# First batch of a frequency-domain mixer: the layout of the buffer between the two short sums, turned from channels-inside to columns-inside

## The chip, the cores and the metric

The kernel runs on one core of one Trainium2 chip. The metric is the device time of one execution in microseconds (us). Timings of the kernel before come from three runs; one further execution was taken with the hardware profiler, and every duration below is from that one.

## The reference, cut to what matters

Two blocks run one after the other on `x` of shape (8, 3008, 256), that is batch, sequence, channels, all in float32:

```python
# block 1: a filter along the sequence, in the frequency domain
X = np.fft.rfft(x, axis=1)
Y = X * (filt_r + 1j * filt_i)[None]
y = np.fft.irfft(Y, n=x.shape[1], axis=1)
# block 2: token mixing, then channel mixing
h = np.maximum(y.transpose(0, 2, 1) @ w_tok1, 0.0) @ w_tok2
u = y + h.transpose(0, 2, 1)
out = u + np.maximum(u @ w_ch1, 0.0) @ w_ch2
```

The sequence length 3008 is 47 x 64, and the kernel computes the Fourier transform in two short sums: one of length 64 and one of length 47, each as matrix products with tables of cosines and sines.

## The kernel before, in words

**Batches.** The eight batches go through the frequency filter in groups (0), (1, 2), (3, 4), (5, 6), (7). The filter of batch 0 runs first and alone; its steps share the engines with the reading and conversion of the 64-bit weights. After that, the mixer of one batch runs together with the filter of a later group. The order of instructions on every engine is written out by hand (`tc.manual_schedule()`): generators yield, and a driver loop at the end of the kernel calls them in turn. No planner reorders anything.

**The first batch.** `dft(GROUPS[0])` does it in three parts.

- The sum of length 64 (`a_unit`, line 530): twelve products of the table `wa0` with a tile of `x`, 128 x 512 outputs each, alternating between two PSUM banks. ScalarE copies each result into the SBUF buffer `turned` (line 533). One copy holds four columns of the length-47 sum by 128 channels; the first six copies fill channels 0 to 127, the last six channels 128 to 255.
- The turn (line 621): VectorE transposes `turned` in place, in 32 x 32 blocks, so that the 24 columns of the length-47 sum (padded with zeros to 32 by the memset of line 1192) go to the partitions, and 32 of the frequencies come to the free dimension. Each instruction takes 16 channels, 128 x 512 elements. Eight of them run after the sixth copy, eight after the twelfth.
- The sum of length 47 (`b_unit`, line 642), for k = 0 to 31: TensorE multiplies a table `wb` with the slice `turned[:, k, :]`, 256 channels, as the moving operand. VectorE multiplies the result with the filter (line 647), and `bi_unit` (line 656) goes back with two more products, of the result before (k - 1). ScalarE copies that out of PSUM (line 666), and a DMA takes it to DRAM (line 663).

**What runs between.** ScalarE also doubles the filter's rows (`filt_double`, line 248), prepares a table (`table_turn`, lines 255 and 256) and starts each conversion of a weight tile (line 276). TensorE takes the weight tiles through a product (lines 322 and 323), and ScalarE copies them to their place (line 325). GpSimd and SyncE issue the loads. Half a weight tile is converted for each k.

**The buffer.** `turned` is one SBUF tile of 128 x (32 * 256 + 128) float32. The last 128 elements of a partition hold the table `wa0`. The rest is seen as [partition, slot s of 32, channel d of 256]. The slots are the columns of the length-47 sum before the turn, and the k of `b_unit` after it. The lines that touch it are the view (213), the memset of slots 24 to 31 (1192), the copies (533), the transposes (620 and 621) and the moving operand (642).

A float32 product appears in the profile as two LDWEIGHTS and two MATMUL instructions.

Of the kernel before, what the change touches and what calls it, by code (L numbers as in the profile page):

```python
# [22 lines left out]
D = 256  # L23
P = 128
K2 = 32
# [102 lines left out]
def kernel(  # L128
# [81 lines left out]

    turned = wcp.tile([P, K2 * D + P], FP32, tag="wc", name="turned")
    wa0 = turned[:, K2 * D:]
    turned = turned[:, 0:K2 * D].rearrange("p (s d) -> p s d", d=D)
    chan = []


# [1099 lines left out]
```

## Time and profile before

| what | value |
|---|---|
| median of three runs | 2420.69 us (2418.3 to 2420.76) |
| the profiled execution's own time | 2421.34 us |
| its span, first to last instruction | 2419.5 us |
| TensorE busy / weight loads | 98% / 82% of the span |
| VectorE, ScalarE, GpSimd busy | 80%, 28%, 26% |
| mean granted TensorE clock | 0.996 |
| first batch, length-64 sum | 5.2 to 21.3 us |
| first batch, transposes | 13.7 to 30.9 us |
| first batch, loop over k | 31.0 to 105 us |

A line of a timeline gives the start, the time taken, the engine, the source line, the operation, and output <- input with the number of instructions merged; in brackets stands how long the engine was idle before, and what ended that. A line for a tile or a source line gives the durations as minimum/median/maximum in ns. "PEld" is the load of the stationary operand, which overlaps matmuls. The duration of an instruction runs from its start to its end in the pipeline, so that consecutive instructions overlap by a part of it; the distance between the starts of instructions that follow each other without idle time is what one costs its engine.

### The profile page before, as it was taken

To read this page: it belongs to the slowest core of one execution; us is meant where nothing else is said; L and a number is where in the kernel's file an instruction comes from. 1 tells how busy PE (TensorE), PEld (TensorE's weight loads), DVE (VectorE), ACT (ScalarE), POOL (GpSimd) and SP (SyncE) were. 2 spreads that over 40 slices of the span, in tenths; PEclk is the share of its full clock that TensorE was granted. 3 is DMA by queue.
4 is the path that set the end of the run, shared out by engine and by line. 5 is a ranking of instruction groups with operands and counts; after the bars stand their busy time and mean duration, and the time that the engine had idled before them with its cause. 6 is when DMAs were issued, how large, how long until landed. Compare 5 with 4: busy or idle time off the path is not lost.

```text
span 2419.5 us, 35455 instructions
## 1 busy us (share of the span) xinstructions
PE 2373.8 (98%) x12340; PEld 1984.4 (82%) x12340; DVE 1943.4 (80%) x3668; ACT 686.2 (28%) x1339; POOL 622.8 (26%) x1115
## 2 busy tenths in 40 slices
PE   7989999999999999999999999999999999999998
PEld 4666676978888888987888888897888988898887
DVE  7798778787887888777888888877888777777776
ACT  5733322232221222123222222313222222222222
POOL 7476332113111211211121112112212112112121
PEclk8999999999999999999999999999999999999999
DMA  9985545554343232544344223433434111311100
GB/s 213 248 237 167 156 143 177 158 158 135 111 132 95 80 90 72 168 125 156 101 122 135 79 78 85 125 122 127 125 107 145 57 60 37 114 63 31 39 15 20
DMA packets 186010, 278.64 MB, mean 115 GB/s; under 512 B 35101, under 2 KB 122859, under 8 KB 185832
## 3 DMA queue, kind: packets, MB, share of 16 engines
q1 hardware_dynamic: 139544, 212.56, 28.7%
q0 software_dynamic: 34688, 53.83, 8.2%
q10 hardware_dynamic: 11600, 10.00, 1.4%
q8 instruction: 98, 1.61, 0.3%
q14 instruction: 80, 0.66, 0.1%
HBM read 193.52 MB, written 82.72 MB: 114 GB/s over the span
## 4 chain that ended last, share of the span: by engine, by line
PE 86%; DVE 6%; DMA 4%; issue 2%; POOL 1%; ACT 1%; SPq 0%; ACTq 0%; DVEq 0%; POOLq 0%
PE ps_po L1003 33%; PE ps_pg L969 18%; PE ps_pg L985 14%; PE ps_b L523 4%; PE ps_b L835 3%; PE ps_acc L890 3%; PE ps_acc L835 2%; PE ps_b L890 2%; PE ps_b L868 2%; PE ps_acc L868 2%; PE ps_pg L523 1%; DVE t L947 1%; DMA st<-in_moe_w_tok_dram 1%; DVE hh L947 1%; DMA filt<-in_x_dram 1%
## 5 line engine op out<-in xcount | busy, mean ns | idle before, releaser
L1050 POOL DMA_DIRECT2D out_dram<-r x752 | 409.5, 553 | 1536.5 <-issue 1004.1
L990 ACT ACTIVATE hh<-hh 128x512 f32<-128x512 f32 (+1 forms) x576 | 347.9, 621 | 995.9 <-DVE hh L947 995.9
L947 DVE TENSOR_TENSOR hh<-ps_pg,s 128x512 f32<-128x512 f32 (+3 forms) x864 | 482.5, 586 | 178.3 <-ACT s L972 176.1
L1003 PE MATMUL ps_po<-t,wc 128*128 128x256 f32 (+1 forms) x2304 | 551.4, 379 | 1.8 <-DVE t L947 1.8
L1003 PEld LDWEIGHTS ps_po<-t,wc 128*128 128x128 f32 x2304 | 428.5, 190 | 119.9 <-issue 37.7
L969 PE MATMUL ps_pg<-v,wc 128*128 128x256 f32 (+1 forms) x1728 | 413.3, 375 | 1.6 <-POOL wc L381 1.5
L1003 PE MATMUL ps_po<-hh,wc 128*128 128x256 f32 (+1 forms) x1728 | 413.2, 375 | 1.0 <-POOL wc L382 0.8
L969 PEld LDWEIGHTS ps_pg<-v,wc 128*128 128x128 f32 x1728 | 327.3, 190 | 42.1 <-DVE v L947 3.2
L1003 PEld LDWEIGHTS ps_po<-hh,wc 128*128 128x128 f32 x1728 | 327.8, 190 | 39.6 <-POOL wc L382 2.0
L985 PE MATMUL ps_pg<-u,wc 128*128 128x256 f32 (+1 forms) x1152 | 293.0, 377 | 1.7 <-DVE hh L947 1.6
L947 DVE TENSOR_TENSOR t<-t,hh 128x256 f32<-128x256 f32 (+1 forms) x576 | 246.2, 427 | 19.8
L985 PEld LDWEIGHTS ps_pg<-u,wc 128*128 128x128 f32 x1152 | 216.7, 190 | 45.1 <-DVE hh L947 15.7
L947 DVE TENSOR_TENSOR s<-ps_pg,hh 128x512 f32<-128x512 f32 (+1 forms) x288 | 196.1, 681 | 30.3 <-DVE hh L947 0.5
L972 ACT COPY s<-ps_pg 128x256 f32<-128x256 f32 (+1 forms) x288 | 106.0, 368 | 350.9 <-PE ps_pg L969 348.7
L947 DVE TENSOR_TENSOR t<-hh 128x512 f32<-128x512 f32 (+1 forms) x288 | 195.2, 678 | 0.6 <-ACT hh L990 0.6
L969 PE MATMUL ps_pg<-u,wc 128*128 128x256 f32 (+1 forms) x576 | 169.3, 375 | 3.1 <-DVE hh L947 3.1
L985 PE MATMUL ps_pg<-v,wc 128*128 128x256 f32 (+1 forms) x576 | 168.8, 375 | 0.0
L947 DVE TENSOR_TENSOR u<-ps_acc,u 128x256 f32<-128x256 f32 (+1 forms) x84 | 46.2, 550 | 97.2 <-PE ps_acc L890 66.6
L969 PEld LDWEIGHTS ps_pg<-u,wc 128*128 128x128 f32 x576 | 108.1, 190 | 19.6 <-DVE hh L947 6.4
L985 PEld LDWEIGHTS ps_pg<-v,wc 128*128 128x128 f32 x576 | 109.1, 190 | 12.7
L947 DVE TENSOR_TENSOR u<-ps_b,u 128x512 f32<-128x512 f32 (+2 forms) x126 | 74.5, 591 | 28.8 <-PE ps_b L890 26.7
L890 PE MATMUL ps_acc<-w 128*128 128x256 f32 (+1 forms) x336 | 85.5, 377 | 1.1 <-ACT t L539 1.1
(152 smaller groups left out, 2648.4 us busy)
## 6 DMA issues: line engine op xcount, KB each, us to landing
w<-w_tmp SPq DMA_DIRECT2D x84, 448.0 KB
w<-w_tmp SPq DMA_DIRECT2D x35, 896.0 KB
out_dram<-r POOLq DMA_DIRECT2D x696, 32.0 KB, 2.8
g_tmp<-t SPq DMA_DIRECT2D x112, 192.0 KB
t<-g_tmp SPq DMA_DIRECT2D x42, 512.0 KB
t<-z_tmp SPq DMA_DIRECT2D x180, 96.0 KB
z_tmp<-t SPq DMA_DIRECT2D x60, 256.0 KB
filt<-in_x_dram SPq DMA_DIRECT2D x90, 128.0 KB
```

The lines of the kernel that those rows point to most:

```text
L523: nc.tensor.matmul(outs(i, j), stat(i, j), mov(i, j), start=True, stop=True)
L835: nc.tensor.matmul(ps[:, at], w[:, n], mov, start=(j == 0 and i in (0, 2)), stop=(j == AP - 1 and i >= 5))
L868: nc.tensor.matmul(ps[:, ds(q * P, n)], t4[b, c][:, r, ts(dh, P)], wai[:, 0:n], start=(first and q == 0), stop=(not first and q == 3))
L890: nc.tensor.matmul(ps[:, ds(j * hw, hw)], h1[:, n, :], w2m[m % 2][:, at, 0:hw], start=(i < 2 and j == 0), stop=(j == len(todo) - 1))
L947: nc.vector.tensor_tensor(out=out, in0=in0, in1=in1, op=op)
L969: nc.tensor.matmul(ps[:, 0:hw], chan[0][:, jp, n, :], mov, start=True, stop=True)
L972: nc.scalar.copy(out=s[:, 0], in_=g[0][:, 0, 0:hw])
L985: nc.tensor.matmul(ps[:, 0:hw], chan[0][:, jp, n, :], mov, start=True, stop=True)
L990: nc.scalar.activation(out=hs, in_=hs, func=AF.Relu)
L1003: nc.tensor.matmul(po[i][:, j, 0:hw], chan[1][:, jp, n, :], mov, start=(jp == 0 and first == 1), stop=(jp == JP - 1 and last == 1))
L1050: q.dma_start(bass.AP(tensor=ob.tensor, offset=ob.offset + row * D + g * cw, ap=[[N1 * D, 32], [D if h else -D, n], [1, cw]]), blocks[ts(g ...
```

## The change

The slots come to lie side by side, and the channels 32 elements (128 bytes) apart. Before, the channels lay side by side and the slots 256 elements (1024 bytes) apart. All lines that use the view keep their text; only the addresses change.

```diff
     turned = wcp.tile([P, K2 * D + P], FP32, tag="wc", name="turned")
     wa0 = turned[:, K2 * D:]
-    turned = turned[:, 0:K2 * D].rearrange("p (s d) -> p s d", d=D)
+    turned = turned[:, 0:K2 * D].rearrange("p (d s) -> p s d", s=K2)
     chan = []
```

What each line's access to `turned` looks like within a partition:

| line | access | before | after |
|---|---|---|---|
| 1192 VectorE memset, 8 slots | write | 2048 elements in a row | inner step 128 bytes |
| 533 ScalarE copy, 4 slots x 128 channels | write | runs of 128 elements | inner step 128 bytes |
| 621 VectorE transpose, 16 channels x 32 slots | read and write | inner step 1024 bytes | 512 elements in a row |
| 642 TensorE moving operand, 256 channels | read | 256 elements in a row | step 128 bytes |

The number, the order and the waits of the instructions are the same in both programs, on every engine. No DMA is concerned, as the table `wa0` keeps its place.

## The prediction

> **What bounds the kernel now.** I read the page first, then 10 us windows of the start, then the view of the tile `turned`, then timelines. From the page:
>
> ```profile
> PE   7989999999999999999999999999999999999998
> ...
> PEclk8999999999999999999999999999999999999999
> ```
>
> Each digit is 60.5 us. TensorE is full from the fourth slice on, so later stages pass a delay or a lead of the start on to the end; what counts is when the first batch is done. The only slices with room are the first three. Three windows (start:end, then busy time of PE, PEld, DVE, ACT, POOL, granted clock, DMA share, GB/s):
>
> ```profile
> 20.00:30.00 10.00, 0.68 (x2) 0.00 (x0) 10.00 (x11) 2.81 (x4) 8.73 (x19) 0.59 0.82 189
> ...
> 50.00:60.00 10.00, 10.00 (x37) 7.25 (x36) 7.96 (x15) 8.99 (x16) 8.09 (x15) 1.00 1.04 254
> ...
> 90.00:100.00 10.00, 8.22 (x31) 6.28 (x30) 6.18 (x12) 7.34 (x15) 1.08 (x2) 1.00 0.93 280
> ```
>
> Two different regimes. From 20 to 30 us TensorE stands still while VectorE is full, with eleven transposes in flight. From 38 to 92 us TensorE is full. The instructions on the buffer, in the tile view:
>
> ```profile
> L642 PEld LDWEIGHTS ps_pg<-turned,wb x64: 307/309/338, 30.9 to 101.4; 128*128 128x128 f32 x64
> L642 PE MATMUL ps_pg<-turned,wb x64: 379/394/786, 31.0 to 101.6; 128*128 128x256 f32 x64
> L621 DVE STREAM_TRANSPOSE turned<-turned x16: 1160/1176/1203, 13.7 to 29.7; 128x512 f32<-128x512 f32 x16
> L530 PEld LDWEIGHTS ps_b<-x,turned x12: 186/189/337, 5.2 to 17.2; 128*128 128x128 f32 x12
> ```
>
> The timeline around the turn:
>
> ```profile
> 13.70 17.17 DVE L621 STREAM_TRANSPOSE turned<-turned 128x512 f32<-128x512 f32 x16 [7.49 <-ACT turned L533]
> ...
> 20.71 0.59 ACT L533 COPY turned<-ps_acc 128x512 f32<-128x512 f32 x1 [1.90 <-PE ps_acc L530]
> ...
> 29.13 1.04 ACT L248 COPY filt<-filt 64x1024 f32<-64x1024 f32 x1 [1.47 <-DMA filt<-in_filt_r_dram]
> ...
> 30.76 0.54 ACT L256 ACTIVATE turn_i<-wb 64x192 f32<-64x192 f32 x1
> ...
> 30.97 2.07 PE L642 MATMUL ps_pg<-turned,wb 128*128 128x256 f32 x4 [10.29 <-issue]
> ```
>
> The profile calls TensorE's 10.29 us "issue", but the transposes end at 30.87 and the first product starts 0.1 us later: they held it. The first filter product on VectorE (line 647, at 32.28) also needs line 248 of ScalarE, done at 30.17. That is the next thing late. In the loop over k, TensorE alone:
>
> ```profile
> 51.22 0.61 PE L642 MATMUL ps_pg<-turned,wb 128*128 128x256 f32 x2
> 51.66 0.59 PE L656 MATMUL ps_b<-p,wb 128*96 128x256 f32 x2
> 52.10 0.59 PE L656 MATMUL ps_b<-p,turn_i 128*96 128x256 f32 x2
> 52.53 0.63 PE L642 MATMUL ps_pg<-turned,wb 128*128 128x256 f32 x2
> 52.99 0.59 PE L656 MATMUL ps_acc<-p,wb 128*96 128x256 f32 x2
> 53.42 0.59 PE L656 MATMUL ps_acc<-p,turn_i 128*96 128x256 f32 x2
> 53.85 1.02 PE L322 MATMUL ps_po<-both,wai_t 128*128 128x512 f32 x2
> 54.71 1.02 PE L323 MATMUL ps_po<-both,wai_t 128*128 128x512 f32 x2
> 55.57 0.61 PE L642 MATMUL ps_pg<-turned,wb 128*128 128x256 f32 x2
> ```
>
> No idle time is shown: 4.35 us for two k. From start to start, a pair of 256 columns takes 0.435 to 0.46 us, a pair of 512 takes 0.86; so one instruction costs about 0.217 us for 256 columns, 0.213 of it at 0.83 ns a column (the 0.425 us that a pair of 512 takes more, over 512 columns). ScalarE is close behind with one round in about 4.42 us (line 666 at 39.67 and again, eleven rounds later, at 88.27).
>
> [...] (1) Line 642 loads its weights with a step of 16 bytes: 309 ns, where line 530's 128 columns side by side take 189; against the same loads of line 656 with 96 columns (median 252 to 260 with the step, 163 without) a column costs 0.84 ns without and about 1.7 with it. [...] (2) The transposes, step 1024 bytes on both sides, cost 17.17 / 16 = 1.073 us, 2.1 ns an element; line 1035's transposes, which read a row, have a duration of 671 ns and so a distance of some 0.6 us. (3) ScalarE's line 325 writes 240 elements with a step of 512 bytes in 586 ns; line 972 writes 256 in a row in 373. That is 0.9 ns an element more. [...] No strided moving operand is in this trace. [...]
>
> **The change part by part.**
>
> *Memset (1192).* 1.77 us becomes about 3.7 (2048 x 0.9 more). The three memsets behind it on VectorE move from 6.2 to 8.1 us; the loads that wait for them are issued from 13.2 on, and the first copy into the buffer starts at 7.33, after the memset's end at about 5. Nothing.
>
> *Copies (533).* 512 x 0.9 = 0.46 more, 1.05 us each, twelve: 5.5 us on ScalarE. Six copies started at 7.33 end at 14.15 instead of 13.67 when I chain them with the two banks; the last product waits for its x until 19.58 anyway, so the last copy starts at 20.7 and ends at 21.8 instead of 21.3. On the path: 0.5 us. ScalarE's next instruction (line 276) waits for its data until 26.98 in its second tile, which covers the rest.
>
> *Transposes (621).* 0.61 instead of 1.07 us. The first eight end at 14.2 + 4.9 = 19.1, the others at 21.8 + 4.9 = 26.7, against 30.87: 4.2 us earlier. Of this only what line 248 allows arrives: the first filter product can start at 30.2 instead of 32.28. **Gain 2.1 us.** The other 2.1 us lie under ScalarE's wait.
>
> *Moving operand (642).* At 1.67 ns a column instead of 0.83, 256 columns cost 0.427 instead of 0.213: 0.213 more, for 64 instructions 13.7 us. Those of k = 0 and 1 (4 instructions) run before line 248 is done; those of k = 2 run in the half clock, where 1.67 ns is TensorE's own pace. That leaves 58 x 0.213 = 12.4 us in the full stretch. **Loss 12.4 us.** Nothing covers it there: TensorE has no idle time, and becomes the bound by far, 5.2 us for two k against ScalarE's 4.42. From 92 us on it waits today: 1.75 us at 95 and 0.49 at 103, behind line 248 and a buffer that a store releases. A slower loop gives those transfers time: I take 2.2 us back. Nothing else returns, as the loads behind the loop are issued after the last store of the loop (GpSimd waits for it until 109.65), so that they move along. Loss after that: 10.2 us.
>
> Sum: +10.2 - 2.1 = **+8.1 us**. Against the profiled execution's 2421.34: 2429.4; against the median 2420.69, 0.65 lower: 2428.8. I forecast 2429.
>
> *Bounds of the unknown cost.* Below: 0, since addresses that lie apart give no reason for a faster read. Above: VectorE's 2.1 ns a column gives 0.32 more, 18.5 us, sum +14, 2435; if the strided weights and the strided columns of the same product also hinder each other, so that both wait in turn, about 0.43 more each, sum +20, 2441. I take the weight loads' factor, being the same engine's reads.
>
> **The rivals.** A change of under 0.2% (4.8 us) is about what a measurement here cannot tell from none.
>
> *A, half-rate reads, 0.70:* as worked out, 2429, own range 2424 to 2436.
>
> *B, the moving read is free, 0.17, ends on the other side (not slower):* a float32 matmul takes only one column in 0.83 ns. [...] It decides below 0.08 us more per instruction (58 x 0.08 = 4.6, less the gains). Then only the lead of 2.1 us stays, and ScalarE's own pace may take of it: 2419. Against it: three engines' reads and writes pay in this trace.
>
> *C, free reads and the whole lead, 0.06:* ScalarE's wait shortens too as DMA traffic moves, the lead is 4.2 us, and less work falls into the half clock (up to 2 us): 2415, faster.
>
> *D, [...], 0.07:* 2441.
>
> That the change does not do what it says, the transposes staying at 1.07 us, would add 2.1 us to A: 2431, inside its range.
>
> **How the numbers follow.** Slower: A and D, 0.77. Same: B, 0.17. Faster: C, 0.06. The range 2418 to 2436 takes in A nearly whole and B; it leaves out C, D and A's edge, about 0.2.
>
> **What would show it.** Right: transposes at about 690 ns and done at 26 to 27 us; copies of line 533 at about 1.05 us; line 647's first start near 30.2; pairs of line 642 about 0.86 us apart and 5.2 us for two k, with ScalarE waiting for TensorE; the loop's end 8 us later. Wrong: pairs of line 642 still 0.45 us apart, which is B; or a loop that TensorE spends waiting, in which case my 12.4 us are partly hidden.

## The result and the profile after

The changed kernel takes 2427.28 us (median of 8 runs, 2426.36 to 2428.72), against 2420.73 us for the kernel before (8 runs beside it, 2418.3 to 2422.6): +6.55 us, a ratio of 1.0026 with a 95% interval of 1.0017 to 1.0035. It is slower, by about a quarter of a percent. The profiled execution took 2426.66 us, with a span of 2424.9 us; that is 5.3 us more than the profiled execution of before, so the two traces show a little less than the medians do.

The page of the changed kernel, busy tenths of TensorE and granted clock in 40 slices:

```profile
PE   7999999999999999999999999999999999999998
...
PEclk8999999999999999999999999999999999999999
```

The third slice (121 to 182 us) had a digit of 8 and has a 9 now; it has a 9 in the run with the fast turn alone (below) too, so it is no mark of a slower loop. The three windows of the changed kernel (start:end, busy time of PE, PEld, DVE, ACT, POOL, clock, DMA share, GB/s):

```profile
20.00:30.00 10.00, 2.28 (x5) 1.16 (x4) 5.20 (x9) 3.54 (x5) 8.70 (x17) 0.59 0.87 194
50.00:60.00 10.00, 10.00 (x32) 6.88 (x32) 6.48 (x13) 7.69 (x15) 6.20 (x13) 1.00 0.86 220
90.00:100.00 10.00, 10.00 (x32) 6.84 (x31) 6.48 (x12) 7.64 (x14) 1.09 (x2) 1.00 0.90 245
```

VectorE is busy 5.2 us of the first window instead of 10. In the middle TensorE is full as before, but starts 32 matmuls instead of 37; "full" says nothing of the rate. ScalarE falls from 8.99 to 7.69, as its work comes more slowly from TensorE. And the stall near 95 us is gone. The tile view of `turned`:

```profile
L642 PEld LDWEIGHTS ps_pg<-turned,wb x64: 307/309/337, 26.2 to 109.1; 128*128 128x128 f32 x64
L642 PE MATMUL ps_pg<-turned,wb x64: 596/612/787, 26.2 to 109.5; 128*128 128x256 f32 x64
L621 DVE STREAM_TRANSPOSE turned<-turned x16: 668/670/712, 14.2 to 25.5; 128x512 f32<-128x512 f32 x16
...
L533 ACT COPY turned<-ps_b x6: 1014/1052/1062, 7.2 to 18.6; 128x512 f32<-128x512 f32 x6
```

Of the accesses that lost their neighbours, the copies and the moving read take longer, and the one that won them is paid back: transposes fall from 1176 to 670 ns, copies rise from 586 to 1052, the moving read from 394 to 612. The memset keeps its duration of 1765 ns. The strided weight load beside the read stays at 309. The first filter product of the kernel before, and then the timelines of the changed kernel around the turn:

```profile
32.28 0.69 DVE L647 TENSOR_TENSOR p<-ps_pg,filt 128x512 f32<-128x512 f32 x1 [1.41 <-ACT turn_i L256]
```

```profile
21.28 4.87 DVE L621 STREAM_TRANSPOSE turned<-turned 128x512 f32<-128x512 f32 x8 [2.23 <-ACT turned L533]
29.66 0.69 DVE L647 TENSOR_TENSOR p<-ps_pg,filt 128x512 f32<-128x512 f32 x1 [3.52 <-ACT filt L248]
```

The turn ends at 26.15 us instead of 30.87, and VectorE then waits 3.5 us for line 248 of ScalarE. The first filter product starts at 29.66 instead of 32.28. The loop over k:

```profile
52.40 1.04 PE L642 MATMUL ps_pg<-turned,wb 128*128 128x256 f32 x2
53.26 0.61 PE L656 MATMUL ps_b<-p,wb 128*96 128x256 f32 x2
53.71 0.59 PE L656 MATMUL ps_b<-p,turn_i 128*96 128x256 f32 x2
54.14 1.04 PE L642 MATMUL ps_pg<-turned,wb 128*128 128x256 f32 x2
55.00 0.61 PE L656 MATMUL ps_acc<-p,wb 128*96 128x256 f32 x2
...
57.59 1.03 PE L642 MATMUL ps_pg<-turned,wb 128*128 128x256 f32 x2
```

From 52.40 to 57.59: 5.19 us for two k instead of 4.35. A pair of line 642 takes 0.86 us from start to start, where it took 0.44 to 0.47; the other distances in these two k are the same to 0.02 us.

### The profile page after: what moved, and what is told of

It is laid out like the page before. It is cut to its first block, busy times and chain, and to the rows that moved or that the text cites. A ratio compares the mean times of both kernels' runs of the same rounds, so it can differ in the third digit from the quotient of the medians.

```text
span 2424.9 us, 35455 instructions
## 1 busy us (share of the span) xinstructions
PE 2386.6 (98%) x12340; PEld 1988.3 (82%) x12340; DVE 1935.2 (80%) x3668; ACT 692.3 (29%) x1339; POOL 620.1 (26%) x1115
## 4 chain that ended last, share of the span: by engine, by line
PE 89%; DVE 5%; DMA 2%; POOL 1%; ACT 1%; issue 1%; ACTq 0%; DVEq 0%; SPq 0%; POOLq 0%
PE ps_po L1003 33%; PE ps_pg L969 18%; PE ps_pg L985 14%; PE ps_b L523 4%; PE ps_b L835 3%; PE ps_acc L890 3%; PE ps_acc L835 2%; PE ps_b L890 2%; PE ps_b L868 2%; PE ps_acc L868 2%; PE ps_pg L523 1%; DVE t L947 1%; PE ps_pg L642 1%; DVE hh L947 1%; PE ps_b L656 1%
## 5 line engine op out<-in xcount | busy, mean ns | idle before, releaser
L947 DVE TENSOR_TENSOR u<-ps_b,u 128x512 f32<-128x512 f32 (+2 forms) x126 | 74.4, 591 | 28.9 <-PE ps_b L890 26.7
```

The source lines that it names most:

```text
L947: nc.vector.tensor_tensor(out=out, in0=in0, in1=in1, op=op)
```

## The experiments

In the experiments' programs an added line shifts some line numbers: line 642 appears as 643 or 650, line 621 as 622, line 647 as 648, and line 656 as 657 or, in the sweeps, as 666.

### One part alone: the strided read, or the fast turn

The strided read on the kernel before:

```diff
+    flat = turned[:, 0:K2 * D]
     turned = turned[:, 0:K2 * D].rearrange("p (s d) -> p s d", d=D)
...
-            nc.tensor.matmul(..., turned[:, k, :].unsqueeze(1), ...)
+            nc.tensor.matmul(..., flat[:, k::K2].unsqueeze(1), ...)
```

> The kernel before, with the buffer, the copies and the transposes as they were; only line 642 reads its 256 moving columns 128 bytes apart, as the changed kernel does. It reads other elements than the reference needs, so its output is not the reference's; the amounts are the same. Theory (the strided moving read is the whole loss): a pair of line 642 costs 0.86 us instead of 0.45, the loop over k ends some 10 us later than before, the lead of the faster turn is missing, so about 2.1 us slower than the changed kernel and 8 to 9 us slower than before: about 2429. Rival (the loss comes from the slower copies of ScalarE and the changed order of waits, and the read only adds time that is hidden): under 3 us slower than before, below 2424.

Measured: 2428.57 us (2427.2 to 2429.53), ratio to before 1.003 (1.002 to 1.004), +7.9 us. Its matmuls of that line in the view by source line:

```profile
L643 PEld LDWEIGHTS ps_pg<-turned,wb x64: 307/309/337, 29.8 to 109.7; 128*128 128x128 f32 x64
L643 PE MATMUL ps_pg<-turned,wb x64: 596/612/787, 29.8 to 110.2; 128*128 128x256 f32 x64
```

The same durations as in the changed kernel, with copies at 587 ns. The read makes the loss without any of the other parts; the rival is out. The expectation had some 2.1 us more than the changed kernel; the medians differ by 1.3. In part this is the edit's own doing: for the first k it reads no channel of the last transpose, so that line 642 starts at 29.82 us, before the turn ends at 30.69, and the first filter product comes at 31.13, 1.15 us earlier than before. The 7.9 us hold this small lead.

The fast turn on the changed kernel:

```diff
+    flat = turned[:, 0:K2 * D]
     turned = turned[:, 0:K2 * D].rearrange("p (d s) -> p s d", s=K2)
...
-            nc.tensor.matmul(..., turned[:, k, :].unsqueeze(1), ...)
+            nc.tensor.matmul(..., flat[:, K2 * D - D:].unsqueeze(1), ...)
```

> The changed kernel, with its memset, copies and transposes; only line 642 reads 256 columns side by side (the same last 256 elements for every k, so its output is not the reference's). Theory: a pair of line 642 costs 0.45 us again, transposes stay at 0.61 us each and copies at 1.05 us; the first filter product starts near 29.7 us as in the changed kernel, and of that lead of 2.6 us some 2 us arrive: 2418 to 2420, 1 to 3 us faster than before. Rival (the copies and the order of waits are the loss): slower than before by 3 us or more.

Measured: 2419.91 us (2416.87 to 2422.68), ratio 0.9993 (0.9985 to 1.0001).

```profile
L643 PE MATMUL ps_pg<-turned,wb x64: 379/394/787, 27.3 to 99.4; 128*128 128x256 f32 x64
...
30.39 0.69 DVE L648 TENSOR_TENSOR p<-ps_pg,filt 128x512 f32<-128x512 f32 x1 [3.28 <-ACT filt L249]
```

The matmul is back at 394 ns, copies stay at 1.04 us, and the first filter product starts at 30.39 us, not at the expected 29.7. The rival (3 us slower or more) is out. By the interval, the slower copies and the shorter turn together give between no change and 3.6 us; the medians differ by 0.8, less than the 1 to 3 us that were expected. So the loss of the read is shown alone, while a gain of the turn in the whole time is not told apart from none. The medians of the two parts add up to about the whole: +7.9 and -0.8 make +7.1, where the whole change gave +6.55.

### What decides the price of the read

Line 642 reads another pattern for every four k, so that one profile holds them all. The patterns differ in the step and in how many of the elements lie in the same aligned 16 bytes; that this number sets the price was my estimate. Each of the three sweeps is one execution, and only distances inside it are used.

```diff
+            step = (32, 1, 2, 3, 4, 8, 0, 0)[k // 4]
+            run = 2 if k < 28 else 4
+            if step:
+                mov = flat[:, K2 * D - D * step::step].unsqueeze(1)
+            else:
+                mov = flat.rearrange("p (q s e) -> p q s e", s=K2, e=run)[:, :, K2 - 1, :]
```

> The changed kernel; line 642 reads 256 columns in a different pattern for each four values of k: step 32 elements (k 0 to 3), 1 (4 to 7), 2 (8 to 11), 3 (12 to 15), 4 (16 to 19), 8 (20 to 23), pairs of neighbours 64 elements apart (24 to 27), runs of four neighbours 128 elements apart (28 to 31). The data are not the reference's. Theory [...]: pairs of line 642 at 0.86 us for steps 4, 8 and 32, 0.45 us for steps 1 and 2 and for both kinds of runs; step 3, [...] between them, near 0.64. Rival (the step itself is the cost[...]): steps 2 and 3 cost 0.86 us as well, and runs of two cost more than runs of four.

Three of its pairs in TensorE's timeline, each with the line after it, which starts when the pair has cost its time: step 2, step 3 and step 4.

```profile
51.47 0.64 PE L650 MATMUL ps_pg<-turned,wb 128*128 128x256 f32 x2
51.95 0.59 PE L666 MATMUL ps_acc<-p,wb 128*96 128x256 f32 x2
...
59.12 0.85 PE L650 MATMUL ps_pg<-turned,wb 128*128 128x256 f32 x2
59.80 0.60 PE L666 MATMUL ps_b<-p,wb 128*96 128x256 f32 x2
...
68.99 1.07 PE L650 MATMUL ps_pg<-turned,wb 128*128 128x256 f32 x2
69.88 0.61 PE L666 MATMUL ps_b<-p,wb 128*96 128x256 f32 x2
```

| pattern | elements in an aligned 16 bytes | pair of line 642, us |
|---|---|---|
| step 1 | 4 | 0.44 to 0.47 |
| step 2 | 2 | 0.46 to 0.48 |
| pairs, 64 elements apart | 2 | 0.45 to 0.47 |
| runs of four, 128 apart | 4 | 0.45 to 0.46 |
| step 3 | 1.33 | 0.68 to 0.69 |
| step 4 | 1 | 0.89 |
| step 8 | 1 | 0.90 to 0.91 |
| step 32 | 1 | 0.86 (k = 3; 0.88 at k = 2, where the two pairs of line 666 behind it take 0.83 and 0.85, later 0.43) |

Among these patterns the price follows the number of elements in 16 bytes before it follows the step: pairs that lie 256 bytes apart cost what a row costs (0.45 to 0.47 us against 0.44 to 0.47). Two elements in 16 bytes were enough (0.45 to 0.48 us), one cost 0.86 to 0.91, and step 3 lies between (0.68 to 0.69). Counted in 8 or in 32 bytes the table would not order itself so: steps 2 and 4 have one element each in 8 bytes, the pairs and step 4 two each in 32, and 0.46 to 0.48 or 0.45 to 0.47 stands against 0.89. My 0.86 for steps 4 and 8 was 0.03 to 0.05 low, and step 3 came 0.04 above my 0.64.

The second sweep, with the weights of that line side by side:

```diff
-            step = (32, 1, 2, 3, 4, 8, 0, 0)[k // 4]
+            step = (32, 1, 4, 8, 16, 24, 28, 5)[k // 4]
...
-            nc.tensor.matmul(ps, wbs[k // WC][:, 0:2 * P:2, k % WC], mov, ...)
+            nc.tensor.matmul(ps, wbs[k // WC].rearrange("p a b -> p (a b)")[:, 0:P], mov, ...)
```

> As the sweep over patterns, with weights of line 642 that lie side by side instead of 16 bytes apart, and steps of 32 elements (k 0 to 3), 1 (4 to 7), 4 (8 to 11), 8 (12 to 15), 16 (16 to 19), 24 (20 to 23), 28 (24 to 27) and 5 (28 to 31). The data are not the reference's. Theory [...]: weight loads fall from 309 to 190 ns, and pairs of line 642 stay at 0.86 us for all steps from 4 up. Rival (strided weights and strided moving columns hinder each other, which gave steps 4 and 8 the 0.03 to 0.05 us above step 32 in the first sweep): steps 4 and 8 fall to 0.86 us, or all strided ones fall well below it.

Its weight loads, in the view by source line, fall as expected:

```profile
L650 PEld LDWEIGHTS ps_pg<-turned,wb x64: 189/190/338, 27.0 to 109.7; 128*128 128x128 f32 x64
L650 PE MATMUL ps_pg<-turned,wb x64: 379/621/835, 27.0 to 110.1; 128*128 128x256 f32 x64
```

The pairs: 0.85 to 0.89 for step 32 (its first, 0.89, has pairs of line 666 of 0.82 and 0.86 behind it, which later take 0.43), 0.43 to 0.44 for step 1, 0.89 to 0.90 for step 4, 0.90 to 0.91 for step 8. For steps 4, 8 and 32 these are the prices with strided weights to 0.01 us (0.89, 0.90 to 0.91 and, at k = 3, 0.86), so at these steps strided weights and strided columns do not hinder each other; rival D of the prediction, which had them do so, is out. But the theory's "0.86 for all steps from 4 up" is wrong too: step 16 costs 0.84, step 5 0.89, step 28 0.91 to 0.92, and step 24 costs 1.24. A third sweep, with only the steps changed to (6, 7, 12, 20, 24, 25, 30, 32):

> As the second sweep, weights side by side, steps of the moving columns: 6 elements (k 0 to 3), 7 (4 to 7), 12 (8 to 11), 20 (12 to 15), 24 (16 to 19), 25 (20 to 23), 30 (24 to 27), 32 (28 to 31). The data are not the reference's. Theory 1 (the 1.24 us of step 24 belongs to the address step): step 24 costs 1.24 us again at another k, the others 0.84 to 0.92. Theory 2 (multiples of 12 elements, 48 bytes, [...]): 12 costs as much as 24. Rival (it was the time of the run, k 20 to 23, when other traffic was heavy): step 24 near 0.9 us here, step 25 near 1.24.

```profile
70.86 1.44 PE L650 MATMUL ps_pg<-turned,wb 128*128 128x256 f32 x2
72.10 0.63 PE L666 MATMUL ps_acc<-p,wb 128*96 128x256 f32 x2
```

Step 24 costs 1.24 again, at other k (here 16 to 19), in all four pairs: it belongs to the step, and the rival is out. Step 20 costs 1.04, steps 25 and 30 0.91 and 0.95, steps 6, 7 and 12 between 0.87 and 0.90 (0.92 for step 6 at k = 2, with a pair of line 666 of 0.83 behind it), step 32 0.85 to 0.86. So 12 does not pay what 24 pays, and the second theory is out; the first missed in its other half, as 20 and 30 lie above its 0.84 to 0.92. What is special in 20 and 24 elements (80 and 96 bytes) stays open.

### A layout that pays on neither side

If two elements in 16 bytes are enough (0.45 to 0.48 us in the first sweep), channels can lie in pairs with the slots 8 bytes apart. That VectorE and ScalarE would run with pairs as with a row, too, was my estimate. All lines follow, so the result stays the reference's (the edits of the memset, the copies and line 642 are left out here):

```diff
-    turned = turned[:, 0:K2 * D].rearrange("p (s d) -> p s d", d=D)
+    turned = turned[:, 0:K2 * D].rearrange("p (q s e) -> p s q e", s=K2, e=2)
...
-                    v = turned.rearrange("p s d -> p d s")[:, d:d + 16, :]
+                        v = turned.rearrange("p s q e -> p q e s")[:, q:q + 16, e, :]
```

> The kernel before with a third layout that computes the reference: channels in pairs side by side, the slots 8 bytes apart, pairs of channels 256 bytes apart. [...] A transpose takes 16 channels of one parity. Theory [...]: transposes 0.61 us each, line 642 0.45 us a pair, copies of line 533 between 0.59 and 1.05, at the low end; the lead of 2 to 2.6 us remains, 2418 to 2420. Rival (VectorE and ScalarE pay for any step above one element): transposes 1.07 us and copies 1.05 us, the first product no earlier than 32 us, 2421 or more.

Measured: 2419.53 us (2416.21 to 2425.37), ratio 0.9995 (0.9987 to 1.0004). The tile view:

```profile
L643 PE MATMUL ps_pg<-turned,wb x64: 383/392/785, 25.7 to 99.5; 128*128 128x256 f32 x64
L622 DVE STREAM_TRANSPOSE turned<-turned x16: 668/670/712, 14.0 to 24.9; 128x512 f32<-128x512 f32 x16
...
L533 ACT COPY turned<-ps_b x6: 587/605/626, 7.2 to 17.9; 128x512 f32<-128x512 f32 x6
```

All three are at the price of a row to 20 ns, on three engines, as the theory said: 392 ns against 394 for the matmul, 670 against 670 for the transposes, 605 against 586 for the copies. The first filter product starts at 29.47 us, 2.8 earlier than before. In time it is not told apart from before (1.2 us between the medians). It does beat the changed kernel: by 7.7 us between the medians, and the two intervals against before (0.9987 to 1.0004 and 1.0017 to 1.0035) do not touch.

### Where the lead of the fast turn goes

After the turn, ScalarE waits for the data of the second weight tile until about 26.5 us before it comes to line 248. This lets it start only the first tile there:

```diff
                 if i == NXC - 1:
-                    copies()
+                    advance(copy)
+                    copied[0] += 1
```

> The layout in pairs, and one change of order: at the end of the length-64 sum ScalarE starts only the first weight tile's conversion (line 276) and not the second, whose data come at about 26.5 us and hold everything behind it, the four table loads and line 248 included. The second start moves into the loop over k. It computes the reference. Theory (with a fast turn, ScalarE's wait for that tile is what holds the first filter product): line 248 starts at 25 to 26.5 us when the filter's own data are there, the first filter product at 26 to 27.5, two to three us earlier than with the pairs alone; of that about 2 us arrive, 2416 to 2418. Rival (the filter's data are no earlier, or the loop gives the lead back to a later load): first product at 29 us or later, or an end like the pairs alone, 2419 to 2420.

> The kernel before with the same change of order alone. Theory (there the transposes hold the first product until 30.9 us, so ScalarE's wait lies beside them): the first filter product moves from 32.3 to no earlier than 31.7 us, and the time is that of before within 1 us. Rival (ScalarE's wait is a bound by itself): as fast as or faster than the layout in pairs alone, 2 us or more below before.

With the pairs: line 248 starts at 23.39 us and the first filter product at 27.70, held by the matmul before it (line 643, from 26.40 us, with a granted clock of 0.50 from 25 to 30 us); yet the median is 2421.86 us (2417.04 to 2428.06), ratio 1.0003 (0.9995 to 1.0012), and the expected 2416 to 2418 did not come. On the kernel before: the product starts at 32.38 as it did, and the time is 2425.02 us (2423.32 to 2430.54), ratio 1.0016 (1.001 to 1.0023), slower by 3.9 us. Neither its theory nor its rival had that. The timeline of the latter's profile, TensorE and then SyncE:

```profile
79.21 0.59 PE L656 MATMUL ps_b<-p,turn_i 128*96 128x256 f32 x2
84.19 1.21 PE L642 MATMUL ps_pg<-turned,wb 128*128 128x256 f32 x2 [4.39 <-DMA wb<-wbi_t]
```

```profile
75.03 1.47 SPq L343 DMA_DIRECT2D st<-in_moe_w_tok_dram  x2
76.61 4.03 SPq L576 DMA_DIRECT2D wb<-wbi_t  x6
...
SPq L343 <- DMA g_tmp<-t: 6.4, 1, 6.4
```

TensorE waits 4.4 us for a table late in the loop, and runs at half clock for about 3.4 us after it (granted 0.91 from 80 to 85 us and 0.75 from 85 to 90: at 0.50, that is 0.9 and 2.5 us). This execution, at 2425.44 us, is a typical one. SyncE issues that table's load at 76.61 us, where it was issued at 64.17 before. Ahead of it in SyncE's queue stands the last load of a weight tile (line 343), at 75.03 us instead of 62.77, which waited 6.4 us for a store of results (the last line gives its waits from 66 to 76 us: the sum, how many, the longest). So after this change of order a weight tile's load holds back a table that the loop needs. Whether the moved tile or the four table loads bring that about was not tried apart.

With the pairs the cause of the median stays open. The profiled execution took 2417.04 us and is the fastest of the thirteen: TensorE waits 0.6 us at 78 us for a filter product, but keeps its lead and ends 4.5 us (by the spans) ahead of the trace of before. What the slower ones do, up to 11 us later, no trace shows. Line 248 was not a free gain: on the kernel before, the change of order that brings it forward cost 3.9 us.

## Why the prediction was right, point by point

**The sign and the cause** were right: the moving read costs more than the turn gives. The loss shows alone (+7.9 us); the gain shows in the trace, where the first filter product is earlier, but hardly in the time (-0.8 us, not told from none). Rival B, free reads, would have left 0.45 us pairs; they are 0.86. Rival D is excluded by the weights' sweep. C's premise, a shorter wait of ScalarE, came true by only 0.55 of the 2.1 us that it needed.

**The size** was +8.1 us forecast and +6.55 measured. By its terms, from the traces:

- *The read.* 12.4 us forecast; 29 pairs from k = 3 on grew from about 0.455 to 0.86, which is 11.7 us. The doubled time came out to a hundredth; what I took too low is the pair before, where strided weights had already made 0.455 out of 0.435 (0.43 to 0.44 with weights side by side, in the second sweep).
- *The lead.* The turn ended at 26.15 (forecast 26.7), the copies took 1.05 us as said, and the first product came 2.6 us earlier (forecast 2.1). Of this 0.55 us is luck: the weight tile's data arrived at 26.43 instead of 26.98. But the lead was not kept. Line 642 for k = 2 and k = 3, before and then changed:

```profile
34.85 0.89 PE L642 MATMUL ps_pg<-turned,wb 128*128 128x256 f32 x2
...
38.16 0.61 PE L642 MATMUL ps_pg<-turned,wb 128*128 128x256 f32 x2
```

```profile
32.24 1.06 PE L642 MATMUL ps_pg<-turned,wb 128*128 128x256 f32 x2
...
36.83 1.03 PE L642 MATMUL ps_pg<-turned,wb 128*128 128x256 f32 x2
```

  The lead is 2.6 us at k = 2 and 1.3 us at k = 3. The half clock ends at about 35.4 us in both traces (granted 0.50 from 25 to 35 us and 0.96 from 35 to 40 in both); the second pair of line 656 takes 0.85 us in it, from 34.00 us before and from 31.39 changed, and 0.43 after it. So the work that the lead brought forward, from k = 2 on, ran in the half clock, where before most of it ran after it, and half of the lead was left. The prediction's "Gain 2.1 us" carried the whole lead past a half clock whose end did not move.
- *The stalls taken back.* Forecast 2.2. The last product of the loop starts at 111.57 instead of 104.09, +7.5; 11.7 less 1.3 less 7.5 is 2.9. The waits at 95 and 103 us (1.75 and 0.49) are gone, as said; the rest is pairs beside them that had taken up to 0.66 us.
- *"Nothing else returns"* was the step that failed most. The token sums that follow (line 784) start only 5.8 us later. The last product of the loop, the issue of its last store, GpSimd's next issue and the sums, before and then changed:

```profile
104.09 0.59 PE L656 MATMUL ps_acc<-p,turn_i 128*96 128x256 f32 x2
...
105.60 0.31 ACTq L663 DMA_DIRECT2D g_tmp<-t  x1
...
109.65 1.51 POOL L778 DMA_DIRECT2D t<-g_tmp  x3 [8.91 <-DMA g_tmp<-t]
...
111.77 20.96 PE L784 MATMUL ps_b<-t,w 128*128 128x256 f32 x96 [1.53 <-ACT both L276]
```

```profile
111.57 0.59 PE L656 MATMUL ps_acc<-p,turn_i 128*96 128x256 f32 x2
...
112.60 0.31 ACTq L663 DMA_DIRECT2D g_tmp<-t  x1
...
115.38 1.62 POOL L778 DMA_DIRECT2D t<-g_tmp  x3 [7.50 <-DMA g_tmp<-t]
...
117.55 20.88 PE L784 MATMUL ps_b<-t,w 128*128 128x256 f32 x96
```

  The last store is issued 7.0 us later, but GpSimd, which waits for it, goes on 2.8 us after that instead of 4.0, and TensorE's idle 1.5 us before the sums are gone. I had let the loads move along with the loop and not asked whether the waits behind it shrink. They do so in the run with the strided read alone too: from the last product to the sums it takes 6.0 and 6.3 us in these two kernels, but 7.7 before, 8.5 with the fast turn alone and 7.2 with the pairs. Why the store is waited for less long stays open. Lighter traffic does not show there: the DMA share is 0.36 from 105.60 to 109.65 us before and 0.49 from 112.60 to 115.38 changed.
- *The memset* was priced at 3.7 us and has the duration it had (1.77), starting 1.3 us later (2.5 against 1.2). Both hold in all five traces with this layout, which do not explain the later start. Nothing waited for it, so the error cost nothing.

Together: 11.7 - 1.3 - 2.9 - 1.7 = 5.8, against 5.4 us between the spans. The last two terms are differences of starts, so that 5.8 is the delay at the sums by construction. The forecast had 12.4 - 2.1 - 2.2 = 8.1: the read, the stalls and what returns made it 3.1 us too dear, and the lead 0.8 us too cheap, so in part the sum came near by luck.

## What to carry to other kernels

Count how many elements of each access fall into the same 16 bytes, for every engine that touches the buffer. Here the transposes, the copies and the matmul's columns took 1176, 1052 and 612 ns with one; with two they ran as in a row (670, 605 and 392 against 670, 586 and 394), and a layout of pairs gave that to all at once. Where one access must pay, let it be the one beside idle time: 7.4 us less of VectorE's transposes brought the first filter product forward by 2.6 us, as ScalarE's wait lay over the rest, while 11.7 us more of TensorE's matmuls in a full loop left 7.5 us at the loop's end. And a busy share of 100% before and after can hide a rate that fell by a sixth (5.19 us for two k instead of 4.35); compare the distance between starts.

## What the runs showed of the hardware that I had not expected

- The price of this moving operand depends on the step beyond 16 bytes, too: 256 float32 columns cost, in a pair of instructions, 0.84 us at step 16, 0.86 at 32, 0.89 at 4, 0.95 at 30, 1.04 at 20 and 1.24 at 24, each the same to about 0.01 us in all pairs of one sweep from k = 3 on. The step of 128 bytes in the changed kernel is among the cheap ones.
- Weights with a step of 16 bytes (309 ns against 190) cost this loop almost nothing: pairs of step 1 take 0.43 to 0.44 us with weights side by side and 0.44 to 0.47 with strided ones.
- After a wait of 4.4 us in the middle of a full loop (the kernel before with the change of order), TensorE's clock was halved for about 3.4 us (granted 0.91 and 0.75 in the two stretches from 80 to 90 us); pairs of line 656 that otherwise take 0.43 us took 0.86 and 0.85 there, which made the stall dearer than its length. The trace of the fast turn alone has a slower stretch too, after a wait of 2.4 us before the token sums: 46 of their matmuls start in the 11.58 us from 110.42 us on, where the trace of before has 54 in as long a time from 111.77 us on.
